# Attention and two feed-forwards on one core: the steps of the second feed-forward's weight conversion, held behind the last instructions of their slot

## The chip, the cores and the metric

The kernel runs on one core of one Trainium2 chip. The metric is the device time of one execution in microseconds; lower is better. An unchanged kernel was run three times, and one more execution was profiled.

## What is computed

Three operators follow each other over 2304 tokens (4 batches of 576, 8 heads of 64, so rows of 512):

```python
# attention: heads 0-3 see the last 32 keys, heads 4-7 the earlier keys at a stride of 32
scores = np.where(masks, scale * q @ k.T, -1e9)
x = softmax(scores) @ v                             # 2304 x 512
# first feed-forward, 1536 wide
g = x @ w_gate
y = ((g * sigmoid(g)) * (x @ w_val)) @ w_out        # 2304 x 512
# second feed-forward, 768 wide
h = np.maximum(np.maximum(y @ w1, y @ w2), y @ w3)
out = h @ w_out2
```

All inputs are float32 and the weights come in as 64-bit words. Before use, each block of weights (128 x 512) is turned into float32 and split into a high and a low part. A product is then three matmuls: high by high, high by low, low by high.

## The kernel before, in words

**Chunks and slots.** The tokens are cut into five chunks c = 0 to 4 of 480, 480, 448, 448 and 448 tokens. The first feed-forward runs over 60 slots, written (c, f): chunk c, block f = 0 to 11 of its 1536 columns. A slot has three products of 12 large matmuls each on the tensor engine, PE: the gate (`emit_gate`, tile ps_g), the value (`emit_val`, ps_v) and the output of the slot before (`emit_out`, ps_y). Between them stand four operations on other engines: ACT makes `ht` from ps_g (L502, silu), the vector engine DVE multiplies `ht` by ps_v (L509), ACT makes the high part `hh` (L126), and POOL the low part `hl` (L129). ps_g and ps_v share two PSUM buffers, so ps_g of the next slot needs L502 done, and ps_v of the next slot needs L509 done. ps_y of a slot, which comes a slot later, needs `hh` and `hl`.

**What else is written into the slots.** In chunk 0, three `weight_step`s a slot convert the first feed-forward's weights. From chunk 1 on, `w_v` and `w_o` are read back from DRAM (`reload`). Into chunks 0 to 3, the table `fill` writes the attention of the chunk after: blocks on PE with a softmax (L294 to L304, transposes L309, product with v L323), and units of rows on POOL and DVE, where POOL multiplies a row into the only buffer `pr` (L397 for scores, L419 for values) and DVE sums it (L400, L422) before POOL may write the next. Chunk 4 has no attention beside it.

**The conversion of the second feed-forward's weights** is the list `later`, 63 steps. Nine pairs of blocks come first, five steps each (`pair_steps`): a load of both blocks, two calls of `convert` (ACT L151 and L152, DVE L154, L156, L157 and L158), `combine` (DVE L186, L187, L189, POOL L188) and `part` (four high parts on ACT L197, low parts L198, two of them on DVE and two on POOL, and eight stores to DRAM by the queue of SP). Six blocks of the output weight follow, three steps each (`wo2_steps`: load, `convert`, and a split with ACT L218, POOL L219 and two stores). After each slot from chunk 1 on, `due` grows by PACE[c], and steps are written out until their count reaches it. PACE of 0.75, 1.25, 1.75 and 2.5 gives 9, 15, 21 and 18 steps in chunks 1 to 4. All 63 have to be out by slot (4, 9), the seam, where the tiles of the second feed-forward's main loop come in.

**What sets the order on an engine.** The kernel is written as a stream of instructions, and a scheduler with a time model of its own puts each engine's instructions into the order in which they are issued. It takes an instruction early where its model finds the engine free and the inputs ready. So a step that is written late may be issued many slots earlier, and everything behind it on that engine waits for it: each engine issues in order. `tc.issue_after(ins)` draws an edge without a semaphore: the instructions traced inside it that run on the engine of `ins` have to stand behind `ins` there. It is used already by the early softmaxes and some loads.

Of the kernel before, what the change touches and what calls it, by code (L numbers as in the profile page):

```python
# [11 lines left out]
AF = mybir.ActivationFunctionType  # L12
ALU = mybir.AluOpType
# [15 lines left out]
NP = NT // (2 * TB)  # L29
NFP = NF2 // 2  # L30

PACE = [0, 0.75, 1.25, 1.75, 2.5]
NK = DM // 128

ROWS = [0, 15, 30, 44, 58, 72]
# [22 lines left out]
def tile_attention_swiglu_maxout(  # L58
# [11 lines left out]
    nc = tc.nc  # L70
# [6 lines left out]
    def sub(stack, name, bufs, **kw):  # L77
        return stack.enter_context(tc.tile_pool(name=name, bufs=bufs, **kw))
# [21 lines left out]
    def f32(ap):  # L100
        return ap.bitcast(F32)
# [7 lines left out]
    def width(c):  # L109
        return STRIDE * (ROWS[c + 1] - ROWS[c])  # L110
# [10 lines left out]

    def split(hi, lo, src, hi_eng, lo_eng):
        if hi_eng is nc.gpsimd:
            nc.gpsimd.tensor_scalar(hi, src, 1.0, 1.0, ALU.mult, ALU.mult)
        elif hi_eng is nc.scalar:
            nc.scalar.activation(hi, src, AF.Copy)  # L126
        else:
            nc.vector.tensor_copy(hi, src)
        lo_eng.tensor_tensor(lo, src, f32(hi), ALU.subtract)  # L129


    wt = {}
# [79 lines left out]
    def wo2_steps(f):  # L212
        key = (3, f)

        def part():
            w = cvt.pop(key)
            hi = wpool.tile([128, 512], F32R, name="whi", tag="w")
            nc.scalar.activation(hi, w, AF.Copy)  # L218
            nc.gpsimd.tensor_tensor(w, w, f32(hi), ALU.subtract)  # L219
            for p, src in enumerate((f32(hi), w)):  # L220
                nc.sync.dma_start(wo2dr[:, f, p], src)

        return [lambda: load(key, w2[f, :, 3, :]), lambda: convert(key), part]
# [107 lines left out]
    def local_block(g, early=False):  # L331


        def dst(src):
            for c, i0, i1, o in pieces(LR * g[0], LR * (g[-1] + 1)):
                t, w = slice(i0 * STRIDE, i1 * STRIDE), slice(o * STRIDE, (o + i1 - i0) * STRIDE)
                xh, xl = x_tile(c)
                yield xh[:, 0:2, t], xl[:, 0:2, t], src[:, :, w]

        return Block(loc[g[0]:g[-1] + 1], KB, [mask[0 if n % (NI // LR) == 0 else 1] for n in g], dst, early)  # L340

    def strided_block(srcs, b, g, early=False):

        _, rows, nr = ON_PE[b]

        def dst(src):
            for u, n in enumerate(g):
                r0 = min(n * nr, STRIDE - nr)
                su = src[:, :, u * QB:u * QB + nr * rows].rearrange("p a (r i) -> p a r i", i=rows)
                for c, i0, i1, o in pieces(b * NI, b * NI + rows):  # L350
                    def part(t):
                        t = t[:, 2:4, :width(c)].rearrange("p a (i r) -> p a r i", r=STRIDE)
                        return t[:, :, r0:r0 + nr, i0:i1]

                    xh, xl = x_tile(c)
                    yield part(xh), part(xl), su[:, :, :, o:o + i1 - i0]

        return Block(srcs[g[0]:g[-1] + 1], rows * nr, [smask[b]] * len(g), dst, early)

    def pairs(ns):  # L360
        ns = list(ns)
        return [ns[i:i + 2] for i in range(0, len(ns), 2)]
# [125 lines left out]
    def linear(ps, w, x, n):  # L488
        xh, xl = x
        for k in range(NK):  # L490
            ks = slice(k * 128, (k + 1) * 128)
            product(ps, w[0][:, ks], w[1][:, ks], xh[:, k, :n], xl[:, k, :n], k == 0, k == NK - 1)

    hs = {}
    yacc = {}

    def emit_gate(c, f):
        n = width(c)
        ps = gv.tile([128, 512], F32, name="ps_g", tag="gv")
        linear(ps[:, :n], wt["g", f], xt[c], n)  # L500
        t = h_p.tile([128, N], F32, name="ht", tag="ht")[:, :n]
        nc.scalar.activation(t, ps[:, :n], AF.Silu)  # L502
        return t

    def emit_val(c, f, t):
        n = width(c)
        ps = gv.tile([128, 512], F32, name="ps_v", tag="gv")
        linear(ps[:, :n], wt["v", f], xt[c], n)
        nc.vector.tensor_tensor(t, ps[:, :n], t, ALU.mult)  # L509
        hh = h_p.tile([128, N], F32R, name="hh")[:, :n]  # L510
        hl = h_p.tile([128, N], F32R, name="hl")[:, :n]
        split(hh, hl, t, nc.scalar, nc.gpsimd)
        hs[c, f] = (hh, hl)

    def emit_out(c, f):
# [173 lines left out]
    order = first  # L689
# [7 lines left out]
    def step_load(upto):  # L697
        while n_load[0] < min(upto, limit[0]):
            key = order[n_load[0]]
            load(key, source(key))  # L700
            n_load[0] += 1

    def step_cvt():
        if n_cvt[0] < limit[0]:
            convert(order[n_cvt[0]])
            n_cvt[0] += 1

    def step_split(eng):
        if n_split[0] < limit[0]:
            key = order[n_split[0]]  # L710
            split_w(key, nc.vector if n_split[0] < len(first) and n_split[0] % 3 == 0 else eng)
            n_split[0] += 1

    def weight_step():
        step_load(n_cvt[0] + AHEAD)
        step_cvt()
        step_split(nc.gpsimd)

    def reload(n, f):
        t = (wv_p if n == "v" else wo_p).tile([128, 2, 512], F32R, name=f"w_{n}{f}", tag="w")  # L720
        nc.sync.dma_start(f32(t), wdr[n, f])
        wt[n, f] = (t[:, 0], t[:, 1])

    if True:
        blocks = [strided_block(st0, 0, g, True) for g in pairs(range(st0.shape[0]))]
        blocks += [local_block(g, True) for g in pairs(range(EARLY))]
        nc.sync.dma_start(cst, shape_consts)
        for i, blk in enumerate(blocks):
            blk.load()
            if i in RAW_AT:  # L730
                step_load(n_load[0] + 1)
        lag = 4
        for i in range(len(blocks) + lag):
            if i < len(blocks):
                blocks[i].scores()
                blocks[i].softmax(nc.gpsimd if i % 3 == 2 else nc.vector)
            if len(blocks) - 2 <= i < len(blocks):
                step_cvt()
            if i >= lag:
                blocks[i - lag].transpose(nc.vector if i % 3 == 2 else nc.scalar)  # L740
                blocks[i - lag].pv()
        step_split(nc.gpsimd)
        step_split(nc.gpsimd)
        step_load(n_cvt[0] + 2)
        step_cvt()
        for k in range(LEADW):
            weight_step()
        pending = None
        slots = [(c, f) for c in range(NC) for f in range(NF)]
        fill = {}  # L750
        for c in range(1, NC):
            for i, st in enumerate(attention_steps(c)):
                fill.setdefault(i if c == 1 else (c - 1) * NF + i - 2, []).extend(st)
        later = [step for g in range(NFP) for i in range(3) for step in pair_steps(i, g)]
        later += [step for f in range(NF2) for step in wo2_steps(f)]
        due, done = 0.0, 0
        for s, (c, f) in enumerate(slots):
            work = c == 0
            if c > 0:
                reload("v", f)  # L760
                reload("o", f)
            if work:
                weight_step()
            t = emit_gate(c, f)
            if work:
                weight_step()
            emit_val(c, f, t)
            if work:
                weight_step()
            for step in fill.get(s, []):  # L770
                step()
            if c > 0:
                due += PACE[c]
                while later and done < int(due):
                    later.pop(0)()
                    done += 1
            if (c, f) == (NC - 1, SEAM):
                assert not later
                attn.close()
                two = ctx.enter_context(ExitStack())  # L780
                y_p, yr0_p = (sub(two, n, 1, side="right", reuse_waits="tile") for n in ("y", "yr0"))
                ring0_p = sub(two, "ring0", 1, side="right", reuse_waits="tile")
                yr_p = [yr0_p]
                ring_p = [ring0_p]
                y = [split_y(load_y(0, k)) for k in range(2)]
                load_w(0, 0, 0)
            if pending is not None:
                emit_out(*pending)
            pending = (c, f)
        emit_out(*pending)  # L790
# [130 lines left out]
```

## Time and profile before

| | |
|---|---|
| median of three runs | 919.09 us (918.95 to 921.64) |
| the profiled execution, own time | 921.36 us |
| its span, first to last instruction | 919.6 us |
| PE busy | 833.2 us, 91% of the span |
| DVE busy | 557.6 us, 61% |
| ACT busy, POOL busy | 387.3 us, 388.4 us |
| mean granted TensorE clock | 0.954 of full speed |

The page cuts the span into 40 slices of 23 us. DVE shows 9 or more tenths in most of the slices up to 350 us and 2 to 5 tenths from 420 us on. PE shows 4 to 9 tenths up to 440 us, then 9 in all but the last. A share over the whole span thus says little, and the stretches have to be read one by one. Between the slots' multiplications L509, the stretch from 182.8 us (slot (0, 11)) to 455.9 us (slot (3, 0)) holds chunks 1 and 2; the one from 455.9 to 558.6 us holds chunk 3 and the first slots of chunk 4, up to (4, 1).

### The profile page before, as it was taken

Reading aid. Unit: us, or ns where it says so; the run is one execution under the profiler, and the core shown is the slowest. Engines: PE = TensorE matmul, PEld = TensorE weight load, DVE = VectorE, ACT = ScalarE, POOL = GpSimd, SP = SyncE. Lnnn points to the kernel's source line nnn. Section 1 sums busy time; section 2 is a strip of 40 time slices with the busy share of each in tenths; the row PEclk is TensorE's granted clock in tenths of the full one; section 3 lists DMA queues with packets and bytes.
Section 4 is the critical chain, followed back from the end, with each engine's and each line's share of the span. In section 5 each row is a group of like instructions: output and inputs, shape, how many; then the busy total and the mean of one; then the engine's idle time right before and its main releaser. Section 6 shows DMA issues by size and latency. Waiting matters only on the chain.

```text
span 919.6 us, 12606 instructions
## 1 busy us (share of the span) xinstructions
PE 833.2 (91%) x4376; PEld 740.9 (81%) x4376; DVE 557.6 (61%) x1097; ACT 387.3 (42%) x859; POOL 388.4 (42%) x301
## 2 busy tenths in 40 slices
PE   6888979776998876888999999999999999999998
PEld 5767767564877765777999998999999899999996
DVE  3999999999877997874444435001354435442441
ACT  3778676634454734534651324112224312431230
POOL 0455463566766675664547644111121212221110
PEclk9799889995999997998999999999999999999999
DMA  9768758998888785976454456438876556653601
GB/s 236 243 216 295 250 182 285 313 337 298 276 258 296 233 285 172 321 271 219 129 197 130 144 177 212 147 123 326 313 263 240 194 182 229 236 211 115 226 15 69
DMA packets 81774, 203.76 MB, mean 222 GB/s; under 512 B 9484, under 2 KB 50224, under 8 KB 78128
## 3 DMA queue, kind: packets, MB, share of 16 engines
q1 hardware_dynamic: 81712, 202.97, 65.1%
q8 instruction: 35, 0.57, 0.2%
q14 instruction: 27, 0.22, 0.1%
HBM read 161.26 MB, written 41.68 MB: 221 GB/s over the span
## 4 chain that ended last, share of the span: by engine, by line
PE 59%; DVE 21%; DMA 6%; ACT 6%; issue 6%; POOL 1%; SPq 0%; DVEq 0%; ACTq 0%; POOLq 0%
PE ps_a L583 12%; PE ps_z L656 8%; PE ps_c L583 6%; PE ps_g L484 3%; PE ps_g L485 3%; PE ps_g L486 3%; DVE w L157 3%; PE ps_y L484 3%; PE ps_v L484 3%; PE ps_y L486 3%; PE ps_y L485 3%; DVE w L156 3%; PE ps_v L485 3%; PE ps_v L486 3%; PE ps_b L583 3%
## 5 line engine op out<-in xcount | busy, mean ns | idle before, releaser
L129 POOL TENSOR_TENSOR hl<-t,hh 128x384 fp32r<-128x384 f32 x36 | 37.6, 1048 | 208.9 <-ACT hh L126 166.8
L129 POOL TENSOR_TENSOR hl<-ht,hh 128x448 fp32r<-128x448 f32 (+1 forms) x60 | 79.1, 1319 | 107.7 <-ACT hh L126 107.7
L484 PE MATMUL ps_g<-xh,wh_g 128*128 128x448 f32 (+1 forms) x240 | 96.2, 401 | 23.6 <-ACT ht L502 19.0
L484 PE MATMUL ps_v<-xh,w_v 128*128 128x448 f32 (+1 forms) x240 | 94.2, 393 | 10.2 <-DVE ht L509 7.7
L486 PE MATMUL ps_v<-xh,w_v 128*128 128x448 f32 (+1 forms) x240 | 92.3, 385 | 6.4 <-DVE w_v L129 6.4
L486 PE MATMUL ps_g<-xh,wl_g 128*128 128x448 f32 (+1 forms) x240 | 94.7, 394 | 0.8 <-POOL wl_g L129 0.8
L583 PE MATMUL ps_a<-yhT,wr 128*128 128x384 f32 x324 | 94.4, 338 | 0.6 <-ACT s L597 0.6
L485 PE MATMUL ps_g<-xl,wh_g 128*128 128x448 f32 (+1 forms) x240 | 94.3, 393 | 0.0
L397 POOL TENSOR_TENSOR pr<-stk,stq 128x1088 f32<-128x1088 f32 (+17 forms) x44 | 79.3, 1803 | 33.7 <-DVE stsc L400 21.7
L419 POOL TENSOR_TENSOR pr<-stv,stsc 128x1088 f32<-128x1088 f32 (+17 forms) x44 | 74.2, 1686 | 45.6 <-DVE sto L422 32.2
L485 PE MATMUL ps_v<-xl,w_v 128*128 128x448 f32 (+1 forms) x240 | 91.4, 381 | 0.0
L485 PE MATMUL ps_y<-hl,w_o 128*128 128x448 f32 (+1 forms) x240 | 89.2, 377 | 2.4 <-POOL hl L129 2.4
L486 PE MATMUL ps_y<-hh,w_o 128*128 128x448 f32 (+1 forms) x240 | 87.2, 380 | 2.3 <-POOL w_o L129 2.3
L484 PE MATMUL ps_y<-hh,w_o 128*128 128x448 f32 (+1 forms) x240 | 86.9, 383 | 2.2 <-DVE ysb L528 2.2
L509 DVE TENSOR_TENSOR ht<-ps_v,ht 128x448 f32<-128x448 f32 (+1 forms) x60 | 37.9, 631 | 80.5 <-PE ps_v L486 76.5
L597 ACT ACTIVATE s<-ps_a 128x384 f32<-128x384 f32 x81 | 39.4, 490 | 98.9 <-PE ps_a L583 98.7
L484 PEld LDWEIGHTS ps_g<-xh,wh_g 128*128 128x128 f32 x240 | 48.2, 201 | 32.8 <-ACT ht L502 21.7
L126 ACT ACTIVATE hh<-ht 128x448 fp32r<-128x448 f32 (+1 forms) x60 | 35.2, 587 | 83.9 <-DVE ht L509 67.4
L656 PE MATMUL ps_z<-wo2t,hh 128*128 128x512 f32 x216 | 64.8, 392 | 0.9 <-ACT osb L665 0.7
L502 ACT ACTIVATE ht<-ps_g 128x448 f32<-128x448 f32 (+1 forms) x60 | 33.2, 553 | 72.6 <-PE ps_g L486 69.7
L484 PEld LDWEIGHTS ps_v<-xh,w_v 128*128 128x128 f32 x240 | 47.4, 197 | 18.7 <-DVE ht L509 11.0
L583 PEld LDWEIGHTS ps_a<-yhT,wr 128*128 128x128 f32 x324 | 59.7, 188 | 1.6 <-ACT s L597 1.0
(134 smaller groups left out, 2000.6 us busy)
## 6 DMA issues: line engine op xcount, KB each, us to landing
wr<-wsdr SPq DMA_DIRECT2D x27, 1792.0 KB, 7.5
raw<-in_w_dram SPq DMA_DIRECT2D x60, 512.0 KB, 4.8
w_v<-wvdr SPq DMA_DIRECT2D x48, 512.0 KB, 3.9
w_o<-wodr SPq DMA_DIRECT2D x48, 512.0 KB, 4.4
wsdr<-whi SPq DMA_DIRECT2D x27, 256.0 KB, 4.2
wvdr<-w_v SPq DMA_DIRECT2D x12, 512.0 KB, 3.9
wodr<-w_o SPq DMA_DIRECT2D x12, 512.0 KB, 4.9
loct<-in_loc_dram SPq DMA_DIRECT2D x24, 192.0 KB, 6.0
```

The lines of the kernel that those rows point to most:

```text
L126: nc.scalar.activation(hi, src, AF.Copy)
L129: lo_eng.tensor_tensor(lo, src, f32(hi), ALU.subtract)
L397: eng.tensor_tensor(pv, self.k[:, 0:i + 1, :], self.q[:, r:r + 1, :].to_broadcast([128, i + 1, D]), ALU.mult)
L419: eng.tensor_tensor(pv, self.v[:, :, 0:i + 1], self.sc[:, r:r + 1, 0:i + 1].to_broadcast([128, D, i + 1]), ALU.mult)
L484: nc.tensor.matmul(ps, wh, xh, start=first, stop=False)
L485: nc.tensor.matmul(ps, wh, xl, start=False, stop=False)
L486: nc.tensor.matmul(ps, wl, xh, start=False, stop=last)
L502: nc.scalar.activation(t, ps[:, :n], AF.Silu)
L509: nc.vector.tensor_tensor(t, ps[:, :n], t, ALU.mult)
L583: nc.tensor.matmul(ps, wts[:, c, a, ks], y[k][b], start=first and k == q == 0, stop=k == 1 and q == 2, skip_group_check=True,)
L597: nc.scalar.activation(s, self.a, AF.Copy)
L656: nc.tensor.matmul(z[j], a[:, ts], w[:, f, b], start=f == q == 0, stop=f == NF2 - 1 and q == 2)
```

## The change

`split` returns its two instructions, `emit_val` records the slot's L509, `hh` and `hl`, and every step of `later` that is written out in that slot gets three edges: its DVE instructions stand behind that slot's L509, its ACT instructions behind its `hh`, its POOL instructions behind its `hl`. The DMAs of the steps, on SP, get no edge of their own. PACE becomes 1.0, 1.25, 1.5 and 2.25, which gives 12, 15, 18 and 18 steps in chunks 1 to 4. No instruction is added or removed. Line numbers grow by 2 from L502 on and by 5 after the loop; the text keeps the numbers of before.

```diff
-PACE = [0, 0.75, 1.25, 1.75, 2.5]
+PACE = [0, 1.0, 1.25, 1.5, 2.25]
...
     def split(hi, lo, src, hi_eng, lo_eng):
         if hi_eng is nc.gpsimd:
-            nc.gpsimd.tensor_scalar(hi, src, 1.0, 1.0, ALU.mult, ALU.mult)
+            a = nc.gpsimd.tensor_scalar(hi, src, 1.0, 1.0, ALU.mult, ALU.mult)
         elif hi_eng is nc.scalar:
-            nc.scalar.activation(hi, src, AF.Copy)
+            a = nc.scalar.activation(hi, src, AF.Copy)
         else:
-            nc.vector.tensor_copy(hi, src)
-        lo_eng.tensor_tensor(lo, src, f32(hi), ALU.subtract)
+            a = nc.vector.tensor_copy(hi, src)
+        return a.ins, lo_eng.tensor_tensor(lo, src, f32(hi), ALU.subtract).ins
...
-        nc.vector.tensor_tensor(t, ps[:, :n], t, ALU.mult)
+        m = nc.vector.tensor_tensor(t, ps[:, :n], t, ALU.mult).ins
...
-        split(hh, hl, t, nc.scalar, nc.gpsimd)
+        last_val[:] = [m, *split(hh, hl, t, nc.scalar, nc.gpsimd)]
...
             if c > 0:
                 due += PACE[c]
-                while later and done < int(due):
-                    later.pop(0)()
-                    done += 1
+                with ExitStack() as order:
+                    for ins in last_val:
+                        order.enter_context(tc.issue_after(ins))
+                    while later and done < int(due):
+                        later.pop(0)()
+                        done += 1
```

**On DVE, between the L509 of slot (0, 11) and that of slot (1, 0).** `ht_1918` and `ht_1988` are the tiles of these two slots, `w32` and `s12` tiles of the conversion. Before:

```order
L509 TENSOR_TENSOR ht_1918<-ps_v_1920,ht_1918 128x480
L158 ISA w32_2244<-w32_2244,q_2243 128x1024
L154 TENSOR_SCALAR w32_2328<-w32_2328 128x512
L329 TENSOR_TENSOR xl_319<-ps_a_1733,xh_318 128x2x5x12
L156 TENSOR_SCALAR w32_2328<-w32_2328 128x512
L400 TENSOR_REDUCE stsc_1882<-pr_1887 128x14
L157 SCALAR_TENSOR_TENSOR w32_2328<-raw_2135,w32_2328 128x512
L158 ISA w32_2328<-w32_2328,q_2327 128x1024
L186 TENSOR_TENSOR s12_2479<-w32_2328 128x256
L187 TENSOR_TENSOR s12_2479<-s12_2479,w32_2244 128x256
```

Now:

```order
L329 TENSOR_TENSOR xl_319<-ps_a_1733,xh_318 128x2x5x12
L511 TENSOR_TENSOR ht_1918<-ps_v_1920,ht_1918 128x480
L400 TENSOR_REDUCE stsc_1882<-pr_1887 128x14
L400 TENSOR_REDUCE stsc_1882<-pr_1890 128x15
L511 TENSOR_TENSOR ht_1988<-ps_v_1990,ht_1988 128x480
L400 TENSOR_REDUCE stsc_1882<-pr_1950 128x16
```

The first pair's conversion, which is written in chunk 1, stood around these two multiplications (three more rows of it follow before the next L509). It is gone from here: its first row now stands behind the L509 of slot (1, 1), and two reductions of the attention are all that is left between the two.

**On ACT, between `hh` of slot (0, 11) and `hh` of slot (1, 0).** Before:

```order
L126 ACTIVATE hh_1934<-ht_1918 128x480
L197 ACTIVATE whi_2549<-w32_2244 128x512
L197 ACTIVATE whi_2554<-w32_2328 128x512
L197 ACTIVATE whi_2559<-s12_2479 128x512
L502 ACTIVATE ht_1988<-ps_g_1975 128x480
L197 ACTIVATE whi_2564<-s4_2480 128x256
L151 ACTIVATE q_2747<-raw_2629 128x512
L152 ACTIVATE w32_2748<-raw_2629 128x512
L151 ACTIVATE q_2867<-raw_2631 128x512
L530 ACTIVATE ysb_2075<-ps_y_900 128x480
L126 ACTIVATE hh_2004<-ht_1988 128x480
```

Now:

```order
L126 ACTIVATE hh_1934<-ht_1918 128x480
L504 ACTIVATE ht_1988<-ps_g_1975 128x480
L532 ACTIVATE ysb_2079<-ps_y_900 128x480
L126 ACTIVATE hh_2004<-ht_1988 128x480
L532 ACTIVATE ysb_2085<-ps_y_902 128x480
```

Three high parts of converted weights, whose inputs come from DVE and POOL, stood ahead of the silu L502; now the silu follows `hh` at once.

**On DVE in chunk 3, between the L509 of slots (3, 3) and (3, 4), as the change has it.** `w32_4410` and `w32_4418` are two blocks of the conversion, `sto` rows of the attention.

```order
L422 TENSOR_REDUCE sto_4501<-pr_4508 128x64
L154 TENSOR_SCALAR w32_4410<-w32_4410 128x512
L156 TENSOR_SCALAR w32_4410<-w32_4410 128x512
L157 SCALAR_TENSOR_TENSOR w32_4410<-raw_4337,w32_4410 128x512
L154 TENSOR_SCALAR w32_4418<-w32_4418 128x512
L422 TENSOR_REDUCE sto_4501<-pr_4566 128x64
L158 ISA w32_4410<-w32_4410,q_4409 128x1024
L156 TENSOR_SCALAR w32_4418<-w32_4418 128x512
L157 SCALAR_TENSOR_TENSOR w32_4418<-raw_4339,w32_4418 128x512
L158 ISA w32_4418<-w32_4418,q_4417 128x1024
L422 TENSOR_REDUCE sto_4501<-pr_4569 128x64
L511 TENSOR_TENSOR ht_4454<-ps_v_4456,ht_4454 128x448
```

Before, no row of a conversion stood between any two L509 of chunk 3; now this slot, the fullest, has eight.

## Rows read from the trace of the kernel before

**Rows 1.** Windows: us; PE, PEld, DVE, ACT, POOL busy (count); PEclk, DMA share, GB/s.

```profile
182.80:221.30 38.50, 23.91 (x123) 18.49 (x123) 37.20 (x66) 17.82 (x43) 24.41 (x16) 0.77 0.96 328
221.30:332.20 110.90, 103.01 (x520) 86.25 (x520) 96.42 (x174) 56.57 (x119) 73.52 (x62) 0.96 0.79 260
332.20:355.80 23.60, 11.84 (x51) 9.72 (x51) 23.36 (x36) 5.19 (x11) 16.03 (x9) 0.81 0.87 298
355.80:455.90 100.10, 89.70 (x439) 79.47 (x439) 64.36 (x133) 51.41 (x109) 58.46 (x51) 0.93 0.66 222
455.90:558.60 102.70, 102.01 (x560) 92.86 (x559) 48.78 (x92) 36.26 (x76) 62.22 (x41) 1.00 0.53 171
565.70:631.30 65.60, 65.60 (x325) 60.57 (x324) 5.61 (x9) 10.13 (x18) 11.16 (x10) 1.00 0.46 155
```

**Rows 2.** Timeline of PE, last value matmul of slot (0, 11): start, us, operation.

```profile
175.99 0.38 PE L486 MATMUL ps_v<-xh,w_v 128*128 128x480 f32 x1
```

**Rows 3.** Timeline of DVE around the L509 of slot (0, 11).

```profile
180.00 2.02 DVE L156 TENSOR_SCALAR w<-w 128x512 int32<-128x512 int32 x1
...
182.81 0.65 DVE L509 TENSOR_TENSOR ht<-ps_v,ht 128x480 f32<-128x480 f32 x1
...
183.97 0.42 DVE L154 TENSOR_SCALAR w<-w 128x512 f32<-128x512 f32 x1
```

**Rows 4.** Timeline of POOL, same moment.

```profile
179.45 2.29 POOL L397 TENSOR_TENSOR pr<-stk,stq 128x896 f32<-128x896 f32 x1
```

**Rows 5.** Lines of DVE, 182.8 to 455.9: busy us, mean ns, idle before.

```profile
L156 DVE TENSOR_SCALAR w<-w 128x512 int32<-128x512 int32 x23 | 27.6, 1202 | 0.4
...
L157 DVE SCALAR_TENSOR_TENSOR w<-raw,w 128x512 int32<-128x512 int32 x24 | 22.9, 956 | 0.4
L158 DVE CUSTOM_DVE_ANT_0 w<-w,q 128x1024 uint16<-128x1024 uint16 x24 | 22.5, 937 | 0.4
L154 DVE TENSOR_SCALAR w<-w 128x512 f32<-128x512 f32 x23 | 17.3, 754 | 4.5 <-ACT w L152 4.5
...
L198 DVE TENSOR_TENSOR w<-w,whi 128x512 f32<-128x512 f32 x9 | 12.3, 1363 | 2.0 <-ACT whi L197 1.7
L198 DVE TENSOR_TENSOR s<-s,whi 128x512 f32<-128x512 f32 x9 | 11.5, 1281 | 2.9 <-ACT whi L197 2.8
L187 DVE TENSOR_TENSOR s<-s,w 128x256 f32<-128x256 f32 x9 | 10.9, 1213 | 0.2
...
L189 DVE TENSOR_TENSOR s<-w,s 128x256 f32<-128x256 f32 x9 | 6.3, 700 | 0.1
L186 DVE TENSOR_TENSOR s<-w 128x256 f32<-128x256 f32 x9 | 4.7, 518 | 0.1
```

**Rows 6.** Line L158, every convert: ns min/median/max, first and last start.

```profile
L158 DVE CUSTOM_DVE_ANT_0 w<-w,q x60: 674/684/2637, 31.0 to 423.4; 128x1024 uint16<-128x1024 uint16 x60
```

**Rows 7.** Waits of PE, 182.8 to 455.9: us in total, times, longest.

```profile
PE ps_g L484 <- ACT ht L502: 16.2, 7, 3.9
...
PE ps_v L484 <- DVE ht L509: 7.0, 6, 2.4
```

**Rows 8.** Timeline of POOL in chunk 1's first slots.

```profile
198.60 2.64 POOL L397 TENSOR_TENSOR pr<-stk,stq 128x1088 f32<-128x1088 f32 x1 [1.19 <-DVE stsc L400]
...
205.83 2.81 POOL L397 TENSOR_TENSOR pr<-stk,stq 128x1152 f32<-128x1152 f32 x1 [3.26 <-DVE stat L297]
```

**Rows 9.** Lines of DVE in chunk 3, 455.9 to 558.6.

```profile
L422 DVE TENSOR_REDUCE sto<-pr 128x64 f32<-128x448 f32 (+11 forms) x12 | 11.8, 984 | 14.0 <-POOL pr L419 13.8
L400 DVE TENSOR_REDUCE stsc<-pr 128x9 f32<-128x576 f32 (+9 forms) x10 | 10.5, 1052 | 8.8 <-POOL pr L397 8.6
```

**Rows 10.** Lines of POOL, 182.8 to 455.9.

```profile
L198 POOL TENSOR_TENSOR w<-w,whi 128x512 f32<-128x512 f32 x9 | 13.5, 1499 | 5.8 <-ACT whi L197 5.7
L198 POOL TENSOR_TENSOR s<-s,whi 128x256 f32<-128x256 f32 x9 | 8.4, 938 | 0.3 <-ACT whi L197 0.3
...
L188 POOL TENSOR_TENSOR w<-w,w 128x256 f32<-128x256 f32 x9 | 8.0, 889 | 5.2 <-DVE stat L303 3.1 <-DVE s L186 1.4 <-DVE stat L302 0.7
```

More of the change, by code (lines that the diff above doesn't have):

```diff
@@ L494, in tile_attention_swiglu_maxout @@
     hs = {}
+    last_val = []
     yacc = {}
```

## Prediction

> **What bounds the kernel now.** I read the windows between the L509 of chosen slots first, because the shares of the whole span mix stretches with different limits. In them, look at PE's busy time against the stretch's length, at DVE's, and at the clock. In 565.7 to 631.3 us, nine slots of chunk 4 with nothing beside them, PE is busy all the time at clock 1.00 [rows 1]: 65.6/9 = 7.29 us is the floor of a slot of 448 tokens, and 7.29 x 480/448 = 7.81 that of one of 480. In chunk 3, 102.7 us for 13 slots, PE is still full; the 560 matmuls are 468 large ones (36 a slot) and 92 of the attention, so one of those costs (102.7 - 13 x 7.29)/92 = 0.086 us. Chunks 1 and 2 are different. I call 182.8 to 221.3 A, 221.3 to 332.2 B, 332.2 to 455.9 C and 455.9 to 558.6 D. A to C hold 25 slots and 123 + 520 + 51 + 439 = 1133 matmuls, 900 of them large. Their floor is 12 x 7.81 + 13 x 7.29 + 233 x 0.086 = 208.5 us, and they take 273.1: **64.6 us above the floor**. PE idles 14.6 + 7.9 + 11.8 + 10.4 = 44.7 of these (length less busy, row by row); the other 20 are matmuls at a lower granted clock (0.77, 0.81 and 0.93, where D has 1.00).
>
> Next, who is full there: DVE, 37.2 of 38.5 and 23.36 of 23.6 us in the two worst stretches, and 96.4 of 110.9 in B. The groups of DVE's lines in A to C show with what: the conversion's nine groups are 136.0 of 221.3 us [rows 5]. It is done at 423.4 us, where the last L158 starts [rows 6], though the program writes it out until slot (4, 9). The waits of PE name the way this reaches it: 16.2 us for L502, 7.0 for L509 [rows 7]. One place in full: slot (0, 11)'s value product starts its last matmul at 175.99 and is done by 176.4 [rows 2], but its L509 starts at 182.81, behind conversion steps such as the L156 of 2.02 us [rows 3].
>
> **The change, part by part.** No operation goes or comes; the question is which stand ahead of a slot's L502, L509 and split.
>
> *What leaves A to C.* The new pace writes out 27 steps there: five pairs and one `convert`. By the mean durations [rows 5], a `convert` is 1.202 + 0.956 + 0.937 + 0.754 = 3.85 us of DVE, and a pair twice that and 1.363 + 1.281 + 1.213 + 0.700 + 0.518 = 5.08, so 12.77. Hence 5 x 12.77 + 3.85 = 67.7 us stay, DVE falls from 221.3 to 85.3 + 67.7 = 153, and in some 220 us it is 70% busy. What stays also stands behind a slot's L509, with most of a slot until the next L509 is due. So the 64.6 us are on the table, and about 3 more ahead of A, since the L509 at 182.81 came some 6 us late [rows 2, 3] and not all of this can be had (bounds 0 and 6).
>
> *What I leave standing*, between nothing and what is lost today:
> - PE's idle time in A was not the conversion's alone. The attention's own chain on POOL runs there, two L397 of 2.64 and 2.81 us ahead of a softmax [rows 8]. I leave 6 of the 14.6.
> - The clock after such a wait: 2 us, between 0 and what it costs in A today: 23.91 us busy against a floor of 2 x 7.81 + 51 x 0.086 = 20.0, so 3.9.
> - B and the rest of C, 23 slots: B's floor is 10 x 7.81 + 7.29 + 124 x 0.086 = 96.0 us for its 11 slots, so it loses 14.9, or 1.35 a slot, with DVE 87% busy. The eleven of 355.8 to 455.9 us lose 100.1 - (11 x 7.29 + 43 x 0.086) = 16.2, or 1.5 a slot, with DVE only 64% busy, and chunk 3 loses nothing at 47%. So it isn't fullness alone, it is what stands ahead of an L509. Upper bound: today's 1.4 a slot, 32 us; lower: 0. I take 7, near the lower, for chunk 3 is the nearest row: no slot there has a conversion step ahead of its L509 that is older than the slot, and the new order allows none either.
> - D gets 18 steps: the rest of pair six and three more pairs, 3.85 + 5.08 + 3 x 12.77 = 47.2 us. DVE goes from 48.8 to 96.0 of 102.7, POOL from 62.2 to 62.2 + 4 x 3.33 = 75.5 (3.33 from [rows 10]). PE was full here, so D can only lose. Upper bound: B's 1.35 a slot, 18 us; lower: 0. I take 7, since DVE is fuller than in B but in the new order.
> - Chunk 4: 18 steps of the output weight, 6 x 3.85 = 23 us of DVE over eight slots where DVE has 0.6 a slot [rows 1]; with the seam, 1 us (0 to 3).
>
> ACT's and POOL's steps are moved with DVE's; ACT was busy 131 of 273 us in A to C [rows 1], so its edges cost only order, and I count them at nothing: what hides them is that the high parts now follow `hh` and wait for DVE anyway. If that cover fails, an L502 waits behind one L197, which the 16.2 us of today already contain. The loads and stores on SP have no edges; DMA is at 66 to 96% in A to C and at 53% in D, and stores that move to D find it emptier, so I count nothing.
>
> *Sum.* 64.6 + 3 - (6 + 2 + 7 + 7 + 1) = **44.6 us** off the profiled execution's 921.4, so 876.8. That execution is 2.3 us above the median of 919.1, so the forecast is **874**. With B to D together between 6 and 22 in place of 14, this case covers 866 to 882.
>
> *A row to weigh.* An L154 alone takes 0.42 us [rows 3], and its mean is 0.754 [rows 5]; the L156 of 2.02 us ran from 180.00 to 182.02 beside an L397 on POOL from 179.45 to 181.74 [rows 3, 4]. So DVE's prices above are prices beside POOL, and they grow where POOL is busier: that is a rival, below. The Trainium skill ("SBUF — State Buffer", section "Who interferes with whom") says that DVE and GpSimd share a pair of ports by an exclusive lock, so that a DVE operation with two inputs in SBUF, or in a two-port mode, and one of GpSimd take turns. The row agrees; by that rule alone the sum would be the first rival's 887 in place of 874.
>
> **The rivals.**
>
> *DVE and POOL take turns in chunk 3* (0.23). If the conversion's DVE steps can't run while POOL works, D needs POOL's 75.5 and 47.2 of conversion, 122.7 us, and not the 109.7 that I give it: 13 more, **887** (882 to 899). For it: the stretched L156. Against it: means already contain some of this, and in A to C the same sum is 150.1 + 67.7 = 218 us (POOL's 172.4, less four pairs at 3.33 and six low parts of the output weight at the 1.499 of an L198 of that size), which binds nothing in 220.
>
> *Almost nothing waits* (0.14). With the steps behind the L509, B, C, D and chunk 4 run at the floor, and only A's 8 us stay: 23 - 8 = 15 less, **859** (852 to 866). For it: D ran at the floor with 48.8 us of DVE. Against it: DVE at 93% there.
>
> *Slower: the attention's handshake behind the conversion* (0.04). POOL writes `pr`, DVE sums it, and only then may POOL write again; DVE waits for it today with a free queue, 13.8 and 8.6 us in chunk 3 [rows 9]. With conversion steps standing between two sums in DVE's order, POOL waits for them and DVE then for POOL, so that the two hardly overlap. A to D hold 153 + 96 = 249 us of DVE and 150.1 + 75.5 = 226 of POOL. They last 375.8 us now, so it decides from where under 99 us of POOL's time (44%) overlap with DVE. Today at least 270.1 + 234.6 - 375.8 = 129 of 234.6 do (55%). At 35%, A to D take 475 - 79 = 396, 20 more than now: **940**. Against it: the steps between are of about 1 us, and DVE's total falls in A to C.
>
> *Today's waits stay* (0.05): B to D lose at the upper bounds of 32 and 18, 36 more than I leave, **910** (899 to 916). Against it: nothing of the conversion is left ahead of the L509 that it delayed. *Nothing happens* (0.01): the scheduler had reached the same times another way, 919. The order in which the engines issue speaks against it: the rows did move.
>
> **How the numbers follow.** The forecast 0.53, turns 0.23, nothing waits 0.14, today's waits 0.05, slower 0.04, nothing 0.01. The range of 857 to 899 takes in the forecast's own range, the first rival and most of the second, and leaves some 0.15 out, today's waits and the slower case above all. A measurement of this kernel can tell about 0.3%, 2.8 us, from no change. Faster by more than that: 0.53 + 0.23 + 0.14 + 0.05 = 0.95; within it 0.01; slower 0.04.
>
> **What the profile after would show.** The last L158 starts in the middle of chunk 4 or later, not at 423.4 us. A to C take some 220 us, with DVE at about 70%, PE idle some 6 in A and the clock near 1.00 in all of them. PE's waits for L502 fall from 16.2 to a few us. D is longer than 102.7 by about 7, with DVE over 90%. I am wrong if D takes 120 us or more (then the turns decide), if DVE's waits for `pr` grow where POOL waits for L400 and L422 (the handshake), or if A still loses its 14.6 us, which would make the stall the attention's own.

## The result and the profile after

The changed kernel takes **885.69 us** (median of three, 885.05 to 886.12) against 919.09: a ratio of 0.9627, 95% interval 0.96 to 0.9655. The forecast of 874 was 12 us too low; the time lies inside the range of 857 to 899, but outside the forecast's own 866 to 882: it falls into the 882 to 899 of the first rival, next to its 887.

The profiled execution took 886.12 us with a span of 884.3. First its windows, cut as those of [rows 1] between the L509 of the same slots, which is now L511 (columns as there). The last one is again nine slots of chunk 4, (4, 2) to (4, 11).

```profile
183.40:206.30 22.90, 19.40 (x105) 16.30 (x105) 12.91 (x34) 9.48 (x26) 15.50 (x9) 0.95 0.95 341
206.30:304.30 98.00, 97.27 (x517) 82.42 (x514) 68.56 (x147) 49.14 (x102) 64.75 (x55) 0.98 0.67 221
304.30:313.40 9.10, 9.10 (x58) 8.09 (x57) 7.93 (x13) 4.17 (x9) 3.86 (x3) 1.00 1.01 340
313.40:407.00 93.60, 91.53 (x496) 80.76 (x495) 69.73 (x145) 48.00 (x105) 64.05 (x52) 1.00 0.75 250
407.00:524.70 117.70, 106.35 (x534) 94.13 (x534) 93.48 (x139) 47.55 (x96) 76.10 (x51) 0.94 0.74 242
530.70:596.90 66.20, 66.03 (x326) 60.78 (x325) 27.34 (x43) 24.40 (x47) 23.38 (x19) 1.00 0.67 222
```

Row by row against [rows 1]: A went from 38.5 to 22.9 us, B from 110.9 to 98.0, C from 123.7 to 102.7. A to C together are 223.6 us in place of 273.1, DVE is busy 159.1 of them (71%), and PE idles 6.3 where it idled 44.7. D went the other way, from 102.7 to **117.7 us**: PE idles 11.4 us where it idled 0.7, and the granted clock is 0.94 where it was 1.00. Of the 15.0 us, 10.7 are idle time, and 4.3 are matmuls that take longer (busy 106.35 us for 534 of them, 102.01 for 560 before). Chunk 4 hardly noticed its 18 steps, 66.2 us for nine slots against 65.6.

The waits of PE in A to C (us in total, times, longest), which answer to [rows 7]:

```profile
PE ps_a L309 <- POOL sm L304: 3.5, 2, 2.5
...
PE ps_g L484 <- ACT ht L504: 0.3, 1, 0.3
...
PE ps_v L484 <- DVE ht L511: 0.2, 1, 0.2
```

16.2 us for the silu and 7.0 for the multiplication have become 0.3 and 0.2. The same view in D:

```profile
PE ps_a L429 <- DVE sto L422: 4.9, 2, 4.4
PE ps_v L484 <- DVE ht L511: 2.4, 1, 2.4
PE ps_g L484 <- ACT ht L504: 2.2, 1, 2.2
PE ps_g L484 <- ACT xh L440: 1.2, 1, 1.2
```

The longest, 4.4 us, is at the start of chunk 4: the last rows of its own attention come too late. How they do is seen in three timelines (start us, length, operation, idle time before it). DVE:

```profile
502.18 2.04 DVE L186 TENSOR_TENSOR s<-w 128x256 f32<-128x256 f32 x1
...
504.63 0.86 DVE L187 TENSOR_TENSOR s<-s,w 128x256 f32<-128x256 f32 x1
505.53 0.84 DVE L189 TENSOR_TENSOR s<-w,s 128x256 f32<-128x256 f32 x1
506.30 1.27 DVE L422 TENSOR_REDUCE sto<-pr 128x64 f32<-128x1088 f32 x1
...
508.09 2.92 DVE L198 TENSOR_TENSOR s<-s,whi 128x512 f32<-128x512 f32 x1
510.93 1.34 DVE L422 TENSOR_REDUCE sto<-pr 128x64 f32<-128x1152 f32 x1
```

POOL at the same time:

```profile
501.55 2.39 POOL L419 TENSOR_TENSOR pr<-stv,stsc 128x1088 f32<-128x1088 f32 x1 [2.94 <-DVE sto L422]
503.90 1.31 POOL L129 TENSOR_TENSOR hl<-ht,hh 128x448 fp32r<-128x448 f32 x1
505.18 0.91 POOL L188 TENSOR_TENSOR w<-w,w 128x256 f32<-128x256 f32 x1
507.65 2.82 POOL L419 TENSOR_TENSOR pr<-stv,stsc 128x1152 f32<-128x1152 f32 x1 [1.56 <-DVE sto L422]
```

And PE:

```profile
512.33 0.42 PE L429 MATMUL ps_a<-cst,sto 128*64 128x128 f32 x1 [4.41 <-DVE sto L422]
513.90 0.74 PE L484 MATMUL ps_g<-xh,wh_g 128*128 128x448 f32 x1 [1.15 <-ACT xh L440]
```

POOL's row is complete at 503.94, but its sum L422 starts at 506.30, behind L186, L187 and L189. L186 takes 2.04 us, and ends at 504.22, 0.28 us after the row that ran on POOL; L187 and L189 take twice their time (0.86 and 0.84 us, 0.41 alone) beside `hl` and L188. Only when that sum is done, at 507.57, does POOL start its next row, at 507.65. That one holds an L198 for 2.92 us, until 0.54 us after its own end at 510.47, and the last sum waits behind it. Then PE, idle since its last matmul, transposes the row.

So two things stand in series: a conversion operation on DVE does not get through while a POOL operation runs (I call that **the hold**), and the sum behind it in DVE's queue releases POOL's next row (the handshake). Which of the two sets the price, the experiments 3 and 5 tell.

### The profile page after: what moved, and what is told of

The parts are those of the page before. It is cut to its first block, busy times and chain, and to the rows that moved or that the text cites. A ratio compares the mean times of both kernels' runs of the same rounds, so it can differ in the third digit from the quotient of the medians.

```text
span 884.3 us, 12555 instructions
## 1 busy us (share of the span) xinstructions
PE 827.2 (94%) x4376; PEld 735.9 (83%) x4376; DVE 554.1 (63%) x1097; ACT 388.7 (44%) x861; POOL 386.2 (44%) x301
## 4 chain that ended last, share of the span: by engine, by line
PE 49%; DVE 21%; DMA 9%; POOL 8%; ACT 6%; issue 6%; SPq 1%; DVEq 0%; ACTq 0%; POOLq 0%
PE ps_a L585 12%; PE ps_z L658 8%; PE ps_c L585 6%; POOL pr L397 4%; PE ps_b L585 3%; DVE w L157 3%; DVE w L156 3%; PE ps_g L484 2%; DVE stsc L400 2%; PE ps_g L486 2%; PE ps_g L485 2%; PE ps_v L484 2%; PE ps_v L485 2%; PE ps_v L486 2%; DVE w L154 2%
## 5 line engine op out<-in xcount | busy, mean ns | idle before, releaser
L484 PE MATMUL ps_g<-xh,wh_g 128*128 128x448 f32 (+1 forms) x240 | 94.2, 392 | 9.7 <-ACT ht L504 5.6
L486 PE MATMUL ps_v<-xh,w_v 128*128 128x448 f32 (+1 forms) x240 | 92.1, 384 | 6.0 <-DVE w_v L129 6.0
L484 PE MATMUL ps_v<-xh,w_v 128*128 128x448 f32 (+1 forms) x240 | 92.4, 385 | 5.2 <-DVE ht L511 2.8
L486 PE MATMUL ps_y<-hh,w_o 128*128 128x448 f32 (+1 forms) x240 | 86.5, 377 | 2.2 <-POOL w_o L129 2.2
L397 POOL TENSOR_TENSOR pr<-stk,stq 128x1088 f32<-128x1088 f32 (+17 forms) x44 | 76.8, 1746 | 26.7 <-DVE stsc L400 24.6
L484 PE MATMUL ps_y<-hh,w_o 128*128 128x448 f32 (+1 forms) x240 | 85.8, 380 | 0.3 <-ACT w_o L126 0.2
L126 ACT ACTIVATE hh<-ht 128x448 fp32r<-128x448 f32 (+1 forms) x60 | 35.3, 588 | 109.5 <-DVE ht L511 107.9
L511 DVE TENSOR_TENSOR ht<-ps_v,ht 128x448 f32<-128x448 f32 (+1 forms) x60 | 37.8, 630 | 39.7 <-PE ps_v L486 35.6
L484 PEld LDWEIGHTS ps_g<-xh,wh_g 128*128 128x128 f32 x240 | 47.2, 197 | 18.2 <-ACT ht L504 7.3
L400 DVE TENSOR_REDUCE stsc<-pr 128x17 f32<-128x1088 f32 (+17 forms) x44 | 37.8, 860 | 31.9 <-POOL pr L397 31.9
```

What stands on the lines that cost most here:

```text
L126: a = nc.scalar.activation(hi, src, AF.Copy)
L397: eng.tensor_tensor(pv, self.k[:, 0:i + 1, :], self.q[:, r:r + 1, :].to_broadcast([128, i + 1, D]), ALU.mult)
L400: nc.vector.tensor_reduce(self.sc[:, r, 0:i + 1], pv, AX.X, ALU.add)
L484: nc.tensor.matmul(ps, wh, xh, start=first, stop=False)
L486: nc.tensor.matmul(ps, wl, xh, start=False, stop=last)
L511: m = nc.vector.tensor_tensor(t, ps[:, :n], t, ALU.mult).ins
```

## The experiments

Twelve kernels were run, each beside the kernel before on the same chip; their ratios are to that, and to be read beside the change's 0.9627. "Chunk 3's stretch" is D, from the L509 (L511) of slot (3, 0) to that of (4, 1).

**1. Is it the edges or the pace?** First the pace alone, in the kernel before:

```diff
-PACE = [0, 0.75, 1.25, 1.75, 2.5]
+PACE = [0, 1.0, 1.25, 1.5, 2.25]
```

> The kernel before with the new PACE alone and no edges. Theory (it is the order that the edges force, and the pace only says in which chunk a step may be written): the scheduler still takes the steps early, so 919 us within 6, with the last convert near 423 us and 13 or more us of PE's idle time between slots (0, 11) and (1, 1). Rival (the three steps fewer in chunk 3 and the gentler pace do it): 890 us or less.

Measured: 921.83 us, ratio 1.0005 (0.9989 to 1.0021). Its convert line, and its first and fifth windows:

```profile
L158 DVE CUSTOM_DVE_ANT_0 w<-w,q x60: 674/683/2650, 31.4 to 423.5; 128x1024 uint16<-128x1024 uint16 x60
```

```profile
183.10:221.50 38.40, 23.16 (x122) 18.06 (x122) 37.12 (x65) 17.73 (x43) 24.32 (x16) 0.81 0.96 325
456.10:559.20 103.10, 102.04 (x560) 92.87 (x560) 49.69 (x93) 36.26 (x76) 62.07 (x41) 1.00 0.50 171
```

The last convert is at 423.5 us as before [rows 6], and every stretch is as before. Without edges the slot in which a step is written means nothing here. Then the edges with the old pace:

```diff
-PACE = [0, 1.0, 1.25, 1.5, 2.25]
+PACE = [0, 0.75, 1.25, 1.75, 2.5]
```

> The edges with the old PACE, so 9, 15, 21 and 18 steps in chunks 1 to 4. Theory: the edges alone bring most of it; three steps more in chunk 3, where 18 steps now cost 17 us above the floor (about 1 us a step), and three fewer in chunks 1 and 2, where 27 cost 11 (0.4 a step): 886 + 3 - 1 = 888 us, with 885 to 892 as bounds. Rival (the pace is half of it): 900 us or more.

Measured: 879.88 us, ratio 0.956 (0.9537 to 0.9582), faster than the change itself. Its windows of C and D:

```profile
300.70:398.70 98.00, 97.81 (x562) 88.45 (x561) 66.36 (x153) 49.26 (x111) 64.57 (x53) 1.00 0.79 260
398.70:516.40 117.70, 106.24 (x534) 93.46 (x533) 94.30 (x146) 48.02 (x102) 79.79 (x53) 0.94 0.78 261
```

The edges bring everything, and the new pace nothing: its part in the change is a loss, if anything. My price of 1 us a step for the three steps more in chunk 3 did not come (117.7 us with 21 steps as with 18), and C is 4.7 us shorter than in the change.

**2. Which engine's edges?** Two kernels, with the edges of DVE alone and with those of ACT and POOL alone:

```diff
-                    for ins in last_val:
+                    for ins in last_val[:1]:
```

> The changed kernel with the edges of DVE's instructions alone, none for ACT's and POOL's. Theory (DVE's order was the bound, and what ACT and POOL do follows DVE's results): 886 us within 5. Rival (the high parts ahead of L502 on ACT, which gave 16.2 us of PE's waits before, need an edge of their own): 895 us or more.

Measured: 891.69 us, ratio 0.9698 (0.9672 to 0.9724), 0.7 us beyond the theory's bound. PE's waits for L504 are back in part, over chunks 1 to 3:

```profile
PE ps_g L484 <- ACT ht L504: 8.1, 4, 2.8
```

The other half (`last_val[1:]`):

> The changed kernel with the edges of ACT's and POOL's instructions alone, none for DVE's. DVE's edges alone gave 891.7 where all three give 885.7. Theory (any one of the engines in a step's chain holds back the rest of the step, since a step's DVE work waits for ACT's L151 and L152): 884 to 900 us, with the first convert on DVE not before slot (1, 0). Rival (only DVE's own edge keeps DVE's queue free): over 905 us.

Measured: 888.52 us, ratio 0.9634 (0.9604 to 0.9665). No conversion of the second feed-forward stands on DVE before the L511 of slot (1, 1). So a step is held back by links of its chain on other engines too: either half brings most of the gain, and DVE's edge on top of the other two cannot be told from nothing.

**3. A second `pr`.** If POOL's wait for the sum is what costs in chunk 3, a second buffer takes it away:

```diff
-    pr_p = sub(attn, "pr", 1, side="right")
+    pr_p = sub(attn, "pr", 2, side="right")
```

> The changed kernel with two buffers of pr in place of one. Theory (in chunk 3 POOL waits to write the next row until DVE has summed the last one, and DVE sums late because a conversion step stands ahead and itself waits for POOL's row to end): with a second buffer POOL no longer waits for the sum, so the stretch of chunk 3 falls from 117.7 us to 104 to 110, and the total to 872 to 879. Rival (DVE and POOL just take turns, whatever the buffers): the stretch stays at 114 or more and the total at 882 or more.

Measured: 881.64 us, ratio 0.9574 (0.9556 to 0.9592), and chunk 3's stretch 116.0 us. The stretch is on the rival's side (114 or more), and the total 0.4 us short of its 882; the theory's fall to 104 to 110 did not come. Of the 4.3 us between the two spans, 2.7 lie ahead of the first L511 and 1.7 in D. POOL's waits for sums in D did fall, from 21.3 us to 7.5, and the stall ahead of slot (4, 0) is gone (that slot takes 7.8 us, 16.8 in the change), but another wait came in its place, which the waits of PE in that stretch show:

```profile
PE ps_v L484 <- DVE ht L511: 8.6, 5, 4.7
PE ps_a L429 <- DVE sto L422: 2.1, 2, 1.5
```

Why, the timelines of slot (3, 8) tell, DVE and then POOL:

```profile
476.08 2.77 DVE L157 SCALAR_TENSOR_TENSOR w<-raw,w 128x512 int32<-128x512 int32 x1
...
480.61 2.54 DVE L186 TENSOR_TENSOR s<-w 128x256 f32<-128x256 f32 x1
...
483.53 0.62 DVE L511 TENSOR_TENSOR ht<-ps_v,ht 128x448 f32<-128x448 f32 x1
```

```profile
475.72 2.57 POOL L419 TENSOR_TENSOR pr<-stv,stsc 128x1088 f32<-128x1088 f32 x1
480.05 2.81 POOL L419 TENSOR_TENSOR pr<-stv,stsc 128x1152 f32<-128x1152 f32 x1 [1.76 <-DVE sto L422]
```

POOL runs ahead, and now it is the conversion that is held behind POOL's rows (L157 until 0.56 us and L186 until 0.29 us after the end of one), with L511 behind it in DVE's queue; PE's wait of 4.7 us follows this L511. The single buffer was the road that the delay took, not its source.

**4. Steps moved out of chunk 3.** Six of them, then all eighteen, into chunk 4:

```diff
-PACE = [0, 1.0, 1.25, 1.5, 2.25]
+PACE = [0, 1.0, 1.25, 1.0, 3.0]
```

> The changed kernel with PACE 1.0 in chunk 3 and 3.0 in chunk 4: 12, 15, 12 and 24 steps, so six steps leave chunk 3 for chunk 4, where there is no attention. Theory: chunk 3's stretch falls by a third of its 17 us above the floor, to about 112, and chunk 4 takes the six steps within its slots: 880 us, bounds 877 to 884. Rival (every step costs where it stands, 1 us each): chunk 4 grows by 6 and the total stays at 886.

Measured: 875.86 us, ratio 0.951 (0.9476 to 0.9543); D and the rest of chunk 4:

```profile
407.40:516.80 109.40, 102.77 (x540) 90.92 (x539) 81.22 (x124) 42.94 (x88) 72.62 (x48) 1.00 0.66 222
516.80:587.40 70.60, 70.60 (x349) 65.14 (x349) 40.13 (x59) 30.24 (x58) 30.36 (x24) 1.00 0.81 286
```

PE's longest wait in D:

```profile
PE ps_a L429 <- DVE sto L422: 1.9, 1, 1.9
```

D gave back 8.3 us, more than the third of 17; PE's wait ahead of slot (4, 0), 4.4 us in the change, is down to 1.9. Chunk 4 took its 24 steps in 70.6 us, where the change needs 72.2 for 18. With `PACE = [0, 1.0, 1.25, 0.0, 4.5]`:

> The changed kernel with PACE 0 in chunk 3 and 4.5 in chunk 4: 12, 15, 0 and 36 steps. Theory (a step costs beside the attention's rows and nothing where there are none): the stretch of chunk 3 is 101 to 104 us, as before the change, chunk 4's slots stay at 7.3 us, and the total is 868 to 873 us. Rival (36 steps are too many for eight slots): chunk 4's slots grow past 8.5 us and the total is 878 or more.

Measured: 870.26 us, ratio 0.9469 (0.9437 to 0.95).

```profile
407.40:505.70 98.30, 98.30 (x532) 90.05 (x531) 46.89 (x92) 32.48 (x66) 59.70 (x39) 1.00 0.52 175
505.70:582.40 76.70, 74.25 (x359) 68.15 (x358) 61.92 (x85) 39.20 (x75) 38.49 (x30) 0.98 0.92 326
```

D is all PE at clock 1.00. Eighteen steps in chunk 3 thus cost 117.7 - 98.3 = 19.4 us, and in chunk 4, on top of the 18 there, 76.7 - 72.2 = 4.5 us, and 2.4 behind the last L511 (289.9 against 287.5). That profiled execution took 874.14 us, 3.9 above the median; by the medians the move gave 15.4 us, so the steps cost some 4 to 7 in chunk 4. Its slots did not stay at 7.3 us: the ten of them take 7.7 each.

**5. The hold taken away, the work left.** The decisive one keeps as many DVE operations in chunk 3, and about as much DVE time as they take when POOL is idle (29.3 us, 26 by the estimate), but of a kind that is not held:

```diff
+            if free[0]:
+                sums(*[f32(w)] * 4)
...
+                if free[0] and n % 2 == 0:
+                    sums(full)
...
+                        free[0] = c == 3
                         later.pop(0)()
```

> The changed kernel in which the conversion steps of chunk 3 are without their arithmetic on DVE: each of their DVE operations (L154 to L158, L186, L187, L189, and DVE's two low parts L198) is a sum over the same 512 or 256 elements into a spare number, so three pairs and the rest of a fourth are not converted. 48 sums of 0.35 to 0.65 us, some 26 us, which is also what the operations that they replace take when POOL is idle (7 x 2.20 + 4 x 2.62). A sum is never seen to be held while POOL runs. Theory (the hold is what makes chunk 3's steps cost): the stretch falls from 117.7 to 101 to 108 us, the stall ahead of slot (4, 0) is gone, and the total is 870 to 877. Rival (it is DVE's queue, as many instructions ahead of L422 and L511): the stretch stays at 114 or more, the total at 882 or more.

Measured: 869.02 us, ratio 0.9427 (0.9396 to 0.9458), 1 us below the theory's bound; 2.9 us of the gain lie ahead of the first L511 (51.6 us, 54.5 in the change). The 48 sums in its trace (two rows, by operand: times, shortest, median and longest in ns), and chunk 3's window:

```profile
L145 DVE TENSOR_REDUCE dum<-w x44: 406/675/689, 409.0 to 490.0; 128x1 f32<-128x512 f32 x32, 128x1 f32<-128x256 f32 x12
L145 DVE TENSOR_REDUCE dum<-q x4: 674/676/679, 415.7 to 491.8; 128x1 f32<-128x512 f32 x4
```

```profile
405.30:507.80 102.50, 99.61 (x535) 90.29 (x534) 70.22 (x140) 44.92 (x94) 70.51 (x51) 1.00 0.83 277
```

None takes over 0.69 us, though 42 of them start while a POOL operation runs. The stretch loses 15.2 of its 117.7 us with as many operations in DVE's queue. PE waits 1.4 us for the multiplication in it, once, and 0.4 for a sum, ahead of slot (4, 0): the number of instructions in the queue isn't the cause, the hold is. Two things more are changed with it. The high parts on ACT no longer wait for a converted weight, which was not tried alone. And DVE is busy 70.2 us in place of 93.5, since the hold's time is gone from it; no run keeps that time without the hold, so whether the hold costs by the length that it adds to DVE's work or by tying its moments to POOL's is not shown.

**6. A try to change the conversion itself.** L154 and L156 are the fast ones, 0.42 us alone, and I took a strided form to be slower and free of the hold:

```diff
+        wf, wi = f32(w), w
+        if not isinstance(key[0], str):
+            wf, wi = (t.rearrange("p (n two) -> p two n", two=2) for t in (wf, w[:, :]))
```

> The changed kernel, with L154 and L156 of the second feed-forward's convert reading and writing their 512 elements two apart (first the even ones, then the odd), and the same arithmetic. Theory (these two are held off the ports until a POOL operation ends because they run in their fast form, 0.42 us alone, and the strided form is slower alone, some 0.6 us, but is not held): no L154 or L156 of the second feed-forward above 0.8 us, where 27 of 60 L156 have a mean of 1.41 beside POOL now; the sum of L154 and L156 in chunk 3's stretch falls from 18.1 us to about 10, the stretch from 117.7 to about 110, the total to 876 to 881. Rival (contention of any kind of access): they stay stretched beside POOL, and the total is 886 or more.

Measured: 883.64 us, ratio 0.9607 (0.9585 to 0.9629), above the theory's 876 to 881 and below the rival's 886; chunk 3's stretch is 117.3 us. The premise failed, as the strided L156 (L159 there) shows; in the change, its median is 427 ns as well:

```profile
L159 DVE TENSOR_SCALAR w<-w x60: 407/428/2654, 27.4 to 567.4; 128x512 int32<-128x512 int32 x60
```

The strided form is as fast and as much held, so the run tells nothing of the theory. The Trainium skill ("VectorE: DVE Perf Modes", section "What auto-detection actually checks") would have told this beforehand: it asks, for the mode that uses both ports, for one source and a destination in SBUF with outermost dimensions (of more than one element) that are both even or equal, and mine are both 2. The 428 ns agree.

**7. Versions.** No steps in chunk 3 together with the second `pr`, with and without the strided form:

> No steps in chunk 3 and two buffers of pr. Theory: as the run that had the strided operations too, which changed nothing: 868 us within 2. Rival: the strided form gave a part of that, 871 or more.

> No steps in chunk 3, two buffers of pr and the strided L154 and L156 together. Theory (with no conversion in chunk 3 the second buffer has nothing to hurt there, and in chunks 1 and 2 less of DVE is held): 3 to 6 us below the run with no steps in chunk 3 alone, 863 to 868. Rival (what is left in chunks 1 and 2 is PE's own work): no difference to it beyond 2 us.

Measured: 869.09 us (ratio 0.9429, 0.9392 to 0.9467) without and 868.14 (0.9443, 0.9418 to 0.9468) with it. The second is 0.1 us above the theory's 863 to 868 and 2.1 below no steps in chunk 3 alone, with ratios that overlap. So the strided form adds nothing that can be told, and the second buffer can't be told from nothing either: 869.09 against 870.26 with one `pr`. Last, the old pace in chunks 1 and 2, `PACE = [0, 0.75, 1.25, 0.0, 4.9]`:

> The edges with 9, 15, 0 and 39 steps: the old pace in chunks 1 and 2, none in chunk 3, the rest in chunk 4. The edges with the old pace had chunk 2's stretch at 98.0 us, where the changed kernel and the run with no steps in chunk 3 have 102.7. Theory (that is the old pace's doing, as it writes three steps fewer ahead of it): chunk 2's stretch is 98 again, chunk 4's slots take three steps more for 1 to 2 us, and the total is 865 to 869 us. Rival (chance of where a step falls, or chunk 4 is full): chunk 2 back at 102 or chunk 4 longer by 4 or more, 870 us or more.

Measured: 869.8 us, ratio 0.9438 (0.9417 to 0.946), between the theory and the rival. C is 98.1 us again, so its 4.7 us do belong to the pace of chunk 1. D is 101.7:

```profile
400.40:502.10 101.70, 101.70 (x548) 93.17 (x547) 49.31 (x95) 33.15 (x72) 62.58 (x41) 1.00 0.53 179
```

PE has no idle time in it, and 16 matmuls more than with no steps in chunk 3 (532 there): 3.4 us more, 0.21 each, which is the 7.29/36 = 0.20 of a large one. So it is work of PE's own that falls between these two multiplications, and no wait. The part behind the last L511 takes 291.4 us, 3.9 more than in the change, and the total can't be told from the 870.26 of no steps in chunk 3. All these versions stand some 16 us below the change and 50 below the kernel before; the simplest of them is the change with no steps in chunk 3.

## Why the prediction was right, and where it was off

**A to C, right.** Forecast were 64.6 us to gain less 6 + 2 + 7, so 49.6; measured 49.5. PE idles 3.5 us in A (6 forecast), by the same route through POOL's softmax that was named, and the waits for L502 and L509 are gone. That the two numbers agree to 0.1 us is luck: against the prediction's floors (20.0, 96.0 and so 92.5 us) A keeps 2.9 us where 8 were forecast, and B and C keep 12.2 where 7 were. PE idles only 6.3 us of these 15.1; 43 matmuls more than before are recorded between the same multiplications (1176 against 1133), so part of the rest is work that was done elsewhere before. (Counted by tile, 883 of the matmuls of before are large and not 900; that lowers the floor by some 2 us.) The last convert starts at 571 us, in slot (4, 8). That the change does what it says, and by its order, is shown by experiment 1.

**The 3 us ahead of A, half right.** Slot (0, 11) takes 12.8 us in place of 15.7, so the gain is there. But the first L511 of all comes 2.9 us later:

```profile
L511 DVE TENSOR_TENSOR ht<-ps_v,ht x60: 606/624/657, 54.5 to 596.9; 128x448 f32<-128x448 f32 x36, 128x480 f32<-128x480 f32 x24
```

54.5 us, against 51.6 before. In the profiles of the experiments it lies anywhere from 51.1 to 55.3, on either side with and without a given edit, so I take these 3 us for a matter of the execution and not of the change; that is not shown, as they weren't tried by themselves.

**D, mis-sized, and the step that failed.** "I take 7, since DVE is fuller than in B but in the new order": it cost 15.0, of which 7 were forecast. The upper bound of 18 held. Two readings failed in it. A fuller DVE was taken as the price: but DVE was not over 90% full in D, it was 79% (93.48 of 117.7 us), and experiment 5 shows that DVE 69% full with sums in the conversion's place costs nothing like it. And I let two rivals stand apart that meet in one trace. The first (turns, 887) had the hold right and its price wrong: its 47.2 us of conversion are durations with the holding in them. Alone, a convert takes 0.415 + 0.417 + 0.688 + 0.684 = 2.20 us, and 47.2 becomes 26, so that 76 + 26 = 102 us of turns would fit in the stretch. The slower rival (the handshake) is in the trace as well: DVE waits for POOL's row with the conversion, POOL waits for the sum behind it. POOL's waits for sums in D rose from 14.0 us to 21.3, while DVE's waits for `pr` fell from 22.4 to 13.1, where the prediction's sign for the handshake wanted both to grow. It isn't the price either: with two buffers (experiment 3) POOL's waits for sums are 7.5 us and the stretch is still 116.0. So it is the hold that costs, whichever instruction waits behind it, L422 or L511. Why 102 us of turns became 117.7 was followed only at the waits shown above.

Of the lock that the Trainium skill states ("SBUF — State Buffer", section "Who interferes with whom"), the trace shows just that: an operation of DVE that is caught ends a fixed time after POOL's, 0.28 or 0.55 us by its kind for the conversion's. By that page's rule alone I had 887, which is nearer the measured 886 than my 874. In part that is luck: that sum had 122.7 us for D, 5.0 too many, and 3 us of gain ahead of A, 3.6 too many, and the two cancel in part. The run with sums shows that the hold is what costs; that it reaches PE by way of what is queued behind it is read from the waits and timelines.

**Chunk 4 and the seam**, 1 us forecast: slot (4, 1) to the last L511 takes 72.2 us against 72.7, and the rest 287.5 against 288.3. It cost nothing.

**The sum.** 49.5 - 15.0 - 0.6 (the start less slot (0, 11)'s gain) + 1.3 = 35.2, against 35.3 between the spans and 44.6 forecast. Eight us of the difference are D's, 3.6 the start's, and 2.3 came back behind.

**What stays open.** Why twelve steps in chunk 1, and not nine, lengthen chunk 2 by 4.7 us was seen in every run with that pace and one `pr`. The windows show that PE idles 2.1 us of it in the change and 0.2 with the old pace, and the longest wait in it is 1.1 us for an L422; the rest is open. Whether a form of L154 and L156 that is not held would pay in chunks 1 to 3 wasn't settled, as experiment 6 didn't give such a form.

## What to carry to other kernels

Where a scheduler with its own time model may pull work ahead, look at where the work stands on the engine and not where it was written: an edge on one link of a step's chain (DVE's) brought 3.0 of the 3.7%, and a pace without an edge moved nothing. Place filler beside what it doesn't collide with: the same 18 steps cost 19.4 us beside the attention's rows and some 4 to 7 in the next chunk, which has none. And price an operation by its duration alone and its duration beside the other engine separately; a mean of both is right for neither, and a second buffer only moves the wait if the source is such a hold.

## What the runs showed of the hardware

The hold in the changed kernel, from all DVE operations of a line, by what POOL did at their start (medians alone, means beside a running POOL operation):

| DVE operation | alone, us | beside POOL, us (longest) | median end after POOL's end |
|---|---|---|---|
| L156, one input | 0.417 | 1.414 (2.65) | 0.283 |
| L158, two inputs | 0.684 | 1.338 (2.08) | 0.548 |
| L186, two inputs of 256 | 0.426 (once) | 1.517 (2.06) | 0.281 |
| L297 of the softmax in the slots, 2 or 4 elements a partition | 0.159 | 0.924 (2.34) | 0.026 |
| L422, a sum | 0.810 | 1.057 (1.34) | no relation |
| L511, one input from PSUM | 0.624 | 0.636 (0.66) | no relation |

The sums differ in size and not in speed (an L400 over a row of 1152 takes 1.34 us alone, once, and 1.32 to 1.35 beside POOL): they and L511, which reads PSUM, go through. That even L297, on two elements, waits out a row of POOL for 2.34 us was not expected: it is in the softmax's own chain, so a hold can delay the attention with no conversion near.

The hold works the other way too. Of the 131 conversion operations that start beside a POOL operation, six end before it, and then POOL's operation is the long one: a row of 1088 takes 3.36 us (2.55 elsewhere), and this `hl` takes 3.96 us, where the median of its size is 1.33, while DVE runs five conversion operations at their usual length. POOL first, then the last two of the five and the one behind them, which is held and ends 0.55 us after POOL:

```profile
64.61 3.96 POOL L129 TENSOR_TENSOR hl<-ht,hh 128x480 fp32r<-128x480 f32 x1 [3.47 <-ACT hh L126]
```

```profile
66.19 0.68 DVE L158 CUSTOM_DVE_ANT_0 w<-w,q 128x1024 uint16<-128x1024 uint16 x1
66.80 0.69 DVE L157 SCALAR_TENSOR_TENSOR w<-raw,w 128x512 int32<-128x512 int32 x1
67.52 1.60 DVE L158 CUSTOM_DVE_ANT_0 w<-w,q 128x1024 uint16<-128x1024 uint16 x1
```
